# Layer-norm scaling as add of the negated mean and multiply, in place of subtract and multiply

## The chip, the cores and the metric

One core of a Trainium2 chip. The metric is the device time of one execution in microseconds; medians are over the fast runs of a kernel, and all runs told here were in the fast state (the one run timed only once has no state). TensorE, VectorE (DVE), ScalarE (ACT) and GpSimd (POOL) are separate engines. This kernel's program gives each of them a queue that is fixed beforehand, and lets them meet at semaphores (counters that one engine raises and another waits for). In the traces each engine works through its queue in order: the VectorE, ScalarE and GpSimd instructions of the kernel before stand in the same order in the first run told below, in which the long norm on GpSimd takes 821 ns in place of 2286.

## The reference, cut to what matters

Two layers, each an attention with a learned feature map followed by a gated MLP without a nonlinearity, both after a layer norm, on 2048 tokens of width 576 in bf16.

```python
def _layernorm(x, axis=-1, eps=1e-5):
    m = jnp.mean(x, axis=axis, keepdims=True)
    v = jnp.var(x, axis=axis, keepdims=True)
    return (x - m) / jnp.sqrt(v + eps)
...
    x = x + _A_ref(_layernorm(x, axis=-1), A_wqkv, A_w_phi, A_wo)      # attention; phi = softmax(p), softmax(-p) per head of 18
    x = x + _B_ref(_layernorm(x, axis=-1), B_w_gate, B_w_up, B_w_down) # (x Wg * x Wu) Wd, inner width 4608
    # ... and both once more
```

## The kernel before

Tokens are cut into 16 tiles of 128, taken in pairs ("blocks", eight of them). Work is written as small threads, and a list scheduler that runs when the program is built orders all instructions of all engines, using a duration that the author gave each operation.

A layer norm takes statistics on VectorE, `rstd = exp(-0.5 ln(var + eps))` on ScalarE, and then scales. The scaling is one of several alternatives; the scheduler takes the one that by its durations ends first. The last 64 columns are written twice (columns 576 to 639 repeat 512 to 575), hence two instructions per tile. (In all code here, "..." marks a cut.)

```python
boot = not fast and sig[0][0] == "xT" and sig[0][1] == 1      # the 16 norms at the start
...
em = [(lambda e, j=j, a=a, b=b, c=c: e.tensor_scalar(xln[:, sl[j], a:b], x_sb[:, ss[j], c:c + b - a],
        mv[:, sl[j], 0:1], rstd[:, sl[j]:sl[j] + 1], ALU.subtract, ALU.mult)) for a, b, c in ((0, 576, 0), (576, 640, 512))]
yield ("alt", [(eng, [Op(d, em[i], ...) for i, d in enumerate(dur)])
               for eng, dur in (("pool", (800, 200)), ("dve", (340, 100)))[:1 + fast]] + ([("act", act)] if boot else []))
```

So 42 of the norms in the gated stretches can only go to GpSimd, the 16 at the start to GpSimd or ScalarE, and six urgent ones (`fast`) to GpSimd or VectorE. GpSimd also forms a difference of the feature-map softmax (`dd<-psb,mxmn`) and its two products (`dd<-dd,ss`). VectorE also forms the softmax's row sums (`ss<-dd`) and the gated product (`hT<-ps,hT`), which empties the PSUM bank that TensorE needs for its next product:

```python
yield ("ops", "act", [Op(540, (lambda e, gb=gb, p=p: e.copy(hT[:, p, :], ps[:, gb, :])), ...)])
yield ("ops", "dve", [Op(625, (lambda e, ub=ub, p=p: e.tensor_tensor(hT[:, p, :], ps[:, ub, :], hT[:, p, :], ALU.mult)), ...)])
```

Of the kernel before, what the change touches and what calls it, by code (L numbers as in the profile page):

```python
# [7 lines left out]
F32 = mybir.dt.float32  # L8
ALU = mybir.AluOpType
ACTF = mybir.ActivationFunctionType  # L10
# [523 lines left out]
class K:  # L534
# [27 lines left out]
    def alloc(self):  # L562
        nc = self.nc
        A = lambda name, shape, dt: self.stack.enter_context(nc.sbuf_tensor(name, shape, dt))
        AT = lambda name, shape, dt, base: nc.alloc_sbuf_tensor_at(name, shape, dt, offset=base)
        self.ident = A("ident", [128, 128], BF16)
        self.epst = A("epst", [128, 1], F32)
        self.mask9 = A("mask9", [128, NK, GH], BF16)
        self.BD = A("BD", [128, NK, GH, CW], BF16)
        self.kvacc = A("kvacc", [128, NK, KW], F32)  # L570
        self.x_sb = A("x_sb", [128, NS, D], BF16)
        self.xT = A("xT", [128, 5, S], BF16)
        self.Wq = A("Wq", [128, 5, D], BF16)
        self.Wk = A("Wk", [128, 5, D], BF16)
        self.Wv = A("Wv", [128, 5, D], BF16)
        self.Wo = A("Wo", [128, 5, D], BF16)
        self.Wg = A("Wg", [128, 4, FF], BF16)
        self.Wu = A("Wu", [128, 4, FF], BF16)
        self.Wr = A("Wr", [128, FF], BF16)
        self.hT = A("hT", [128, NP, 512], BF16)  # L580
        h0 = nc.lookup_mloc(self.hT).addr
        self.Wraw = AT("Wraw", [128, 5, 2 * D], BF16, h0)
        self.WT = AT("WT", [TW, 2, NT, 128], BF16, h0 + 5 * 2 * D * 2)
        a0 = h0 + 5 * 2 * D * 2 + 2 * NT * 128 * 2
        self.BDphi = AT("BDphi", [TW, NT, TW], BF16, a0)
        self.onesf = AT("onesf", [128, 128], F32, a0 + 1280)
        self.wst = AT("wst", [TW, NT, DH], BF16, a0 + 1280 + 512)
        self.mask = AT("mask", [TW, TW], BF16, a0 + 1280 + 512 + 192)
        self.wdr = A("wdr", [128, self.NWD, CH, D], BF16)
        self.xln = A("xln", [128, 2 * self.NXP, 640], BF16)  # L590
        self.wdx = AT("wdx", [128, CH, D], BF16, nc.lookup_mloc(self.xln).addr + 2560)
        self.st = A("st", [128, 2 * self.NXP, 12], F32)
        self.mv = A("mv", [128, 2 * self.NXP, 2], F32)
        self.lnv = A("lnv", [128, 2 * self.NXP], F32)
        self.rstd = A("rstd", [128, 2 * self.NXP], F32)
        self.nmr = A("nmr", [128, 2 * self.NXP], F32)
        self.psb = A("psb", [128, self.NPS, D], BF16)
        self.mxmn = A("mxmn", [128, self.NPS, 2, H], F32)
        self.dd = A("dd", [128, self.NSM, 2, D], BF16)
        self.ss = A("ss", [128, self.NSM, 2 * H], F32)  # L600
        self.vx = A("vx", [128, self.NVX, H, CW], BF16)
        self.eT = A("eT", [128, self.NET, NK, 128], BF16)
        self.den = A("den", [128, self.NO, H], F32)
        self.oT = A("oT", [128, self.NOT, 5, 128], BF16)
        self.ps = self.stack.enter_context(nc.psum_tensor("ps", [128, 8, 512], F32))
        self.psb16 = [self.ps[:, i, :].bitcast(BF16) for i in range(8)]
        self.sbuf_left = nc.sbuf_bytes_remaining
        sc = self.sc
        sc.pool("xlnp", self.NXP)
        sc.pool("sm", self.NSM)  # L610
        sc.pool("psb", self.NPS)
        sc.pool("vx", self.NVX)
        sc.pool("et", self.NET)
        sc.pool("o", self.NO)
        sc.pool("oT", self.NOT)
        sc.pool("wt", 2)
        sc.pool("wd", self.NWD)
        sc.pool("pb", 8)
        self.vx_of = {}
        self.sm_of = {}  # L620
        self.wt_of = {}
        self.wd_slot = {}
        g = self.tr.dma_group
        self.g_wd = [g("wd%d" % i) for i in range(self.NWD + 1)]
        self.g_xt = [g("xt%d" % i) for i in range(2 * self.NXP)]
        self.g_out = g("out")
        self.g_et = [g("et%d" % i) for i in range(self.NET)]
        self.g_ot = [g("ot%d" % i) for i in range(self.NOT)]
        self.raw_keys = [("mask",), ("BDphi",), ("onesf",), ("wst",), ("WT", 0), ("WT", 1)] + [("Wraw", 0, w_, k_) for w_ in ("q", "k") for k_ in range(5)]
# [187 lines left out]
    def t_ln(self, tiles, sig, fast=False, slot=None):  # L817
        s = self
        x_sb, xln, st, mv, rstd, xT = s.x_sb, s.xln, s.st, s.mv, s.rstd, s.xT
        if slot is None:  # L820
            pair = yield ("acq", "xlnp")
            sl = [2 * pair, 2 * pair + 1]
        else:
            sl = [slot]
        n = len(tiles)
        js = range(n)
        key = lambda name: [(name, sl[j]) for j in js]
        ss = tiles
        ops = []
        for j in js:  # L830
            for h in range(2):
                ops.append(Op(d_dve(288), (lambda e, j=j, h=h: e.bn_stats(st[:, sl[j], 6 * h:6 * h + 6], x_sb[:, ss[j], 288 * h:288 * h + 288])),  # L832
                              reads=[("x", ss[j], 0), ("x", ss[j], 1)], writes=[("st", sl[j], h)]))
        yield ("ops", "dve", ops)
        ops = []
        for j in js:
            ops.append(Op(125, (lambda e, j=j: e.bn_aggr(mv[:, sl[j], :], st[:, sl[j], :])),
                          reads=[("st", sl[j], 0), ("st", sl[j], 1)], writes=[("mv", sl[j])]))
        yield ("ops", "dve", ops)
        s0, s1 = sl[0], sl[0] + n  # L840
        var2 = mv[:, s0:s1, 1:2].rearrange("p a b -> p (a b)")
        yield ("ops", "act", [
            Op(230, (lambda e: e.activation(s.lnv[:, s0:s1], var2, ACTF.Ln, bias=s.epst[:, 0:1], scale=1.0)),
               reads=key("mv") + [("epst",)], writes=key("lnv")),
            Op(205, (lambda e: e.activation(rstd[:, s0:s1], s.lnv[:, s0:s1], ACTF.Exp, scale=-0.5)),  # L845
               reads=key("lnv"), writes=key("rstd"))])
        boot = not fast and sig[0][0] == "xT" and sig[0][1] == 1
        if boot:
            mean2 = mv[:, s0:s1, 0:1].rearrange("p a b -> p (a b)")
            yield ("ops", "dve", [Op(80, (lambda e: e.scalar_tensor_tensor(s.nmr[:, s0:s1], mean2, -1.0, rstd[:, s0:s1], ALU.mult, ALU.mult)),  # L850
                                     reads=key("mv") + key("rstd"), writes=key("nmr"))])
        for j in js:
            act = [Op(d, (lambda e, j=j, a=a, b=b, c=c: e.activation(xln[:, sl[j], a:b], x_sb[:, ss[j], c:c + b - a], ACTF.Identity,
                                                                     bias=s.nmr[:, sl[j]:sl[j] + 1], scale=rstd[:, sl[j]:sl[j] + 1])),
                      reads=[("x", ss[j], 0), ("x", ss[j], 1), ("nmr", sl[j]), ("rstd", sl[j])], writes=[("xln", sl[j])]) for a, b, c, d in ((0, 576, 0, 760), (576, 640, 512, 330))]
            em = [(lambda e, j=j, a=a, b=b, c=c: e.tensor_scalar(xln[:, sl[j], a:b], x_sb[:, ss[j], c:c + b - a], mv[:, sl[j], 0:1], rstd[:, sl[j]:sl[j] + 1],  # L856
                                                                 ALU.subtract, ALU.mult)) for a, b, c in ((0, 576, 0), (576, 640, 512))]
            yield ("alt", [(eng, [Op(d, em[i], reads=[("x", ss[j], 0), ("x", ss[j], 1), ("mv", sl[j]), ("rstd", sl[j])], writes=[("xln", sl[j])]) for i, d in enumerate(dur)])
                           for eng, dur in (("pool", (800, 200)), ("dve", (340, 100)))[:1 + fast]] + ([("act", act)] if boot else []))
        for j in js:  # L860
            tok = slice(128 * ss[j], 128 * ss[j] + 128)
            if fast:
# [3 lines left out]
                                        reads=[("xln", sl[j]), ("ident",)], writes=[("pbd", bank)], excl=[("pb", bank)]) for k in range(5)])  # L866
                yield ("ops", "act", [Op(d_act(640, True), (lambda e, P=P, tok=tok: e.copy(xT[:, :, tok], P[:, 0:640].rearrange("p (k n) -> p k n", k=5))),  # L867
                                         reads=[("pbd", bank)], writes=[("xT", ss[j])], excl=[("pb", bank)])])
# [662 lines left out]
```

## Time and profile before

| | before |
|---|---|
| device time | 1173.97 us (1172.96 to 1175.02, three runs) |
| TensorE, VectorE, ScalarE, GpSimd busy | 1091.9, 612.2, 376.1, 361.5 us |
| start, to the first gated matmul | 130.1 us |
| gated stretch of layer 1 | 523.0 us |
| hand-over and layer 2 | 37.2 + 482.8 us |

The last three rows are read from the trace: the first matmul of the gated MLP, and the first residual add on VectorE after the last block of a layer. The stages fit the windows view, whose columns are the stretch, its length, and then the busy microseconds of TensorE, its weight loads, VectorE, ScalarE and GpSimd. Kernel before:

```profile
130.10:653.10 523.00, 515.69 (x7651) 400.36 (x7652) 279.36 (x567) 163.94 (x376) 181.63 (x146) 1.00 0.43 104
653.10:690.30 37.20, 20.00 (x156) 14.20 (x154) 28.12 (x65) 13.13 (x30) 6.95 (x6) 0.79 0.08 25
690.30:1173.10 482.80, 470.49 (x6972) 361.91 (x6972) 202.96 (x411) 116.19 (x238) 86.94 (x70) 0.99 0.43 109
```

The gated stretches show TensorE idle for 7.3 and 12.3 us only.

### The profile page before, as it was taken

Reading aid. Unit: us, or ns where it says so; the run is one execution under the profiler, and the core shown is the slowest. Engines: PE = TensorE matmul, PEld = TensorE weight load, DVE = VectorE, ACT = ScalarE, POOL = GpSimd, SP = SyncE. Lnnn points to the kernel's source line nnn. Section 1 sums busy time; section 2 is a strip of 40 time slices with the busy share of each in tenths; the row PEclk is TensorE's granted clock in tenths of the full one; section 3 lists DMA queues with packets and bytes.
Section 4 is the critical chain, followed back from the end, with each engine's and each line's share of the span. In section 5 each row is a group of like instructions: output and inputs, shape, how many; then the busy total and the mean of one; then the engine's idle time right before and its main releaser. Section 6 shows DMA issues by size and latency. Waiting matters only on the chain.

```text
span 1173.1 us, 34065 instructions
## 1 busy us (share of the span) xinstructions
PE 1091.9 (93%) x15480; PEld 838.8 (72%) x15480; DVE 612.2 (52%) x1262; ACT 376.1 (32%) x857; POOL 361.5 (31%) x301
## 2 busy tenths in 40 slices
PE   5676899999999999999999589999999999999998
PEld 3554686868778686868777368586868686868685
DVE  6787654646547364736544565462626262534131
ACT  6685331423324151413322232131303131312120
POOL 7885223415344251515331121230403030301000
PEclk9897899999999999999999889999999999999999
DMA  6384118253362727254442301817273535354414
GB/s 170 80 273 169 21 25 219 40 158 71 94 132 45 185 34 193 40 157 68 102 114 69 115 10 31 230 23 200 37 187 51 167 69 150 79 140 97 148 47 132
DMA packets 181034, 128.24 MB, mean 109 GB/s; under 512 B 99354, under 2 KB 179738, under 8 KB 179738
## 3 DMA queue, kind: packets, MB, share of 16 engines
q1 hardware_dynamic: 180890, 126.07, 42.3%
q8 instruction: 121, 1.98, 0.7%
q14 instruction: 23, 0.19, 0.1%
HBM read 100.73 MB, written 2.36 MB: 88 GB/s over the span
## 4 chain that ended last, share of the span: by engine, by line
PE 64%; POOL 12%; DVE 12%; ACT 5%; DMA 4%; issue 1%; SPq 0%; DVEq 0%; POOLq 0%
PE ps L1232 31%; PE ps L1302 19%; POOL xln L856 7%; PE ps L898 6%; DVE ss L965 3%; POOL dd L976 3%; DMA wdr<-in_B_w_down_dram 3%; PE ps L1305 3%; POOL dd L935 3%; PE ps L886 2%; PE ps L1131 2%; DVE x_sb L1179 2%; DVE hT L1280 2%; ACT dd L960 1%; PE ps L1017 1%
## 5 line engine op out<-in xcount | busy, mean ns | idle before, releaser
L1232 PE MATMUL ps<-xT,Wu 64*128 64x256 bf16 x4608 | 592.2, 270 | 6.6 <-DVE hT L1280 5.6
L1232 PE MATMUL ps<-xT,Wg 64*128 64x256 bf16 x4608 | 590.5, 270 | 1.6 <-ACT xT L867 1.6
L1232 PEld LDWEIGHTS ps<-xT,Wu 64*128 64x128 bf16 x4608 | 432.1, 94 | 32.7 <-DVE hT L1280 11.7
L1232 PEld LDWEIGHTS ps<-xT,Wg 64*128 64x128 bf16 x4608 | 426.9, 94 | 30.5 <-issue 3.3
L1278 ACT CAST hT<-ps 128x512 bf16<-128x512 f32 x288 | 166.5, 583 | 545.3 <-PE ps L1232 508.4
L1280 DVE TENSOR_TENSOR hT<-ps,hT 128x512 bf16<-128x512 f32 x288 | 196.6, 688 | 203.6 <-ACT hT L1278 203.1
L856 POOL TENSOR_SCALAR xln<-x_sb,mv,rstd 128x576 bf16<-128x576 bf16 x102 | 145.5, 1432 | 464.0 <-ACT rstd L845 458.9
L1302 PE MATMUL ps<-wdr,hT 128*128 128x512 bf16 x960 | 247.8, 380 | 4.3 <-DMA wdr<-in_B_w_down_dram 3.9
L1232 PE MATMUL ps<-xT,Wr 64*128 64x256 bf16 x1152 | 199.0, 271 | 0.0
L1305 PE MATMUL ps<-wdr,hT 128*128 128x64 bf16 x960 | 185.0, 193 | 1.4 <-ACT hT L1278 1.4
L976 POOL TENSOR_TENSOR dd<-dd,ss 128x576 bf16<-128x576 bf16 x124 | 142.9, 1174 | 129.1 <-ACT ss L972 124.4
L1302 PEld LDWEIGHTS ps<-wdr,hT 128*128 128x128 bf16 x960 | 93.8, 98 | 115.0 <-DMA wdr<-in_B_w_down_dram 7.3
L1327 DVE TENSOR_TENSOR x_sb<-ps,x_sb 128x512 bf16<-128x512 f32 x32 | 21.9, 685 | 199.5 <-PE ps L1305 199.5
L965 DVE TENSOR_REDUCE ss<-dd 128x64 f32<-128x1152 bf16 x64 | 86.2, 1347 | 56.3 <-ACT dd L960 56.0
L935 POOL TENSOR_TENSOR dd<-psb,mxmn 128x576 bf16<-128x576 bf16 x62 | 72.1, 1163 | 122.9 <-DVE mxmn L925 122.9
L1305 PEld LDWEIGHTS ps<-wdr,hT 128*128 128x128 bf16 x960 | 94.0, 98 | 2.0 <-ACT hT L1278 2.0
L1232 PEld LDWEIGHTS ps<-xT,Wr 64*128 64x128 bf16 x1152 | 89.6, 95 | 5.6
L958 ACT ACTIVATE dd<-dd 128x576 bf16<-128x576 bf16 x64 | 43.7, 683 | 65.3 <-DVE dd L944 65.2
L925 DVE TENSOR_REDUCE mxmn<-psb 128x32 f32<-128x576 bf16 x64 | 47.3, 739 | 21.1 <-ACT psb L922 21.1
L922 ACT CAST psb<-ps 128x288 bf16<-128x288 f32 x128 | 46.8, 399 | 33.7 <-PE ps L886 22.8
L1302 PE MATMUL ps<-wdx,hT 128*128 128x512 bf16 x192 | 53.5, 380 | 0.0
L832 DVE BATCH_NORM_STATS2 st<-x_sb 128x6 f32<-128x288 bf16 x128 | 49.3, 445 | 5.7 <-DMA x_sb<-in_A_x_dram 5.4
(85 smaller groups left out, 944.7 us busy)
## 6 DMA issues: line engine op xcount, KB each, us to landing
wdr<-in_B_w_down_dram SPq DMA_DIRECT2D x240, 288.0 KB, 3.7
wdx<-in_B_w_down_dram SPq DMA_DIRECT2D x48, 288.0 KB, 3.6
Wg<-in_B_w_gate_dram SPq DMA_DIRECT2D x4, 1152.0 KB, 12.5
Wu<-in_B_w_up_dram SPq DMA_DIRECT2D x4, 1152.0 KB, 15.3
x_sb<-in_A_x_dram SPq DMA_DIRECT2D x8, 288.0 KB, 3.3
out_dram<-x_sb SPq DMA_DIRECT2D x16, 144.0 KB, 2.3
Wraw<-in_A_wqkv_dram SPq DMA_DIRECT2D x8, 144.0 KB, 3.2
xT<-xln SPq DMA_TRANSPOSE x58, 2.6
```

What stands on the lines that cost most here:

```text
L832: ops.append(Op(d_dve(288), (lambda e, j=j, h=h: e.bn_stats(st[:, sl[j], 6 * h:6 * h + 6], x_sb[:, ss[j], 288 * h:288 * h + 288])), reads= ...
L856: em = [(lambda e, j=j, a=a, b=b, c=c: e.tensor_scalar(xln[:, sl[j], a:b], x_sb[:, ss[j], c:c + b - a], mv[:, sl[j], 0:1], rstd[:, sl[j]:s ...
L898: out.append(Op(61, (lambda e, h=h, k=k, st=(i == 0 and k == 0), sp=(i == 1 and k == 3): e.matmul(s.ps[:, banks[h], 0:N], L[r, k, :], Wm[r ...
L925: ops = [Op(665, (lambda e: e.tensor_reduce(mxmn[:, pz, 0, :], p3, AX.X, ALU.max)), reads=[("psb", pz, 0), ("psb", pz, 1)], writes=[("mx", ...
L935: yield ("alt", [(eng, [Op(dur, (lambda e: e.tensor_tensor(d1, p3, mxb, ALU.subtract)), reads=[("psb", pz, 0), ("psb", pz, 1), ("mx", pz)] ...
L965: Op(1320, (lambda e: e.tensor_reduce(ss[:, sm, :].rearrange("p (b g) -> p b g", b=2), e4, AX.X, ALU.add)), reads=s.ddk(sm, 0) + s.ddk(sm, ...
L976: yield ("alt", [(eng, [Op(dur, (lambda e, ev=ev, rb=rb: e.tensor_tensor(ev, ev, rb, ALU.mult)), reads=s.ddk(sm, br) + [("ss", sm)], write ...
L1232: out.append(Op(54.3, (lambda e, bank=bank, cs=cs, lhsT=lhsT, rhs=rhs, st=st, sp=sp: e.matmul(ps[:, bank, cs], lhsT, rhs, start=st, stop=s ...
L1278: yield ("ops", "act", [Op(540, (lambda e, gb=gb, p=p: e.copy(hT[:, p, :], ps[:, gb, :])), reads=[("gu", gb)], writes=[("hT", p)] + (s.raw ...
L1280: yield ("ops", "dve", [Op(625, (lambda e, ub=ub, p=p: e.tensor_tensor(hT[:, p, :], ps[:, ub, :], hT[:, p, :], ALU.mult)), reads=[("gu", u ...
L1302: ops.append(Op(d_pe(512), (lambda e, lhsT=lhsT, bank=bank, slot=slot, fi=fi, f=f: e.matmul(ps[:, bank, 0:512], lhsT, s.wslot(slot)[:, fi, ...
L1305: ops.append(Op(d_pe(64) + 3, (lambda e, lhsT=lhsT, sl=sl, slot=slot, fi=fi, f=f: e.matmul(ps[:, Z, 64 * sl:64 * sl + 64], lhsT, s.wslot(s ...
```

## The change

The intent: the same value by another pair of operations, `(x + (-m)) * rstd`. The negation is a small new VectorE instruction that runs while ScalarE computes rstd. At the start, ScalarE's alternative makes its own bias and copies the tail instead of computing it twice, and its durations are raised from 760 + 330 to 180 + 860 + 240 ns. GpSimd's durations stay at 800 and 200.

```diff
+        self.nmean = A("nmean", [128, 2 * self.NXP], F32)
...
+        mean2 = mv[:, s0:s1, 0:1].rearrange("p a b -> p (a b)")
+        yield ("ops", "dve", [Op(80, (lambda e: e.tensor_scalar(s.nmean[:, s0:s1], mean2, -1.0, None, ALU.mult)), ...)])
...
-        if boot:
-            ... nmr = -mean * rstd by scalar_tensor_tensor on VectorE
...
-            act = [... two ACTF.Identity activations, durations 760 and 330 ...]
-            em = [... e.tensor_scalar(..., mv[:, sl[j], 0:1], rstd[:, sl[j]:sl[j] + 1], ALU.subtract, ALU.mult) ...]
+            act = [Op(180, ... ACTF.Copy, nmr = nmean * rstd ...), Op(860, ... ACTF.Identity, 576 columns ...),
+                   Op(240, (lambda e, j=j: e.copy(xln[:, sl[j], 576:640], xln[:, sl[j], 512:576])), ...)]
+            em = [... e.tensor_scalar(..., s.nmean[:, sl[j]:sl[j] + 1], rstd[:, sl[j]:sl[j] + 1], ALU.add, ALU.mult) ...]
```

(Lines with "..." inside are cut.)

More of the change, by code (lines that the diff above doesn't have):

```diff
@@ L841, in t_ln @@
         var2 = mv[:, s0:s1, 1:2].rearrange("p a b -> p (a b)")
+        mean2 = mv[:, s0:s1, 0:1].rearrange("p a b -> p (a b)")
+        yield ("ops", "dve", [Op(80, (lambda e: e.tensor_scalar(s.nmean[:, s0:s1], mean2, -1.0, None, ALU.mult)), reads=key("mv"), writes=key("nmean"))])
         yield ("ops", "act", [
@@ L847, in t_ln @@
         boot = not fast and sig[0][0] == "xT" and sig[0][1] == 1
-        if boot:
-            mean2 = mv[:, s0:s1, 0:1].rearrange("p a b -> p (a b)")
-            yield ("ops", "dve", [Op(80, (lambda e: e.scalar_tensor_tensor(s.nmr[:, s0:s1], mean2, -1.0, rstd[:, s0:s1], ALU.mult, ALU.mult)),
-                                     reads=key("mv") + key("rstd"), writes=key("nmr"))])
         for j in js:
-            act = [Op(d, (lambda e, j=j, a=a, b=b, c=c: e.activation(xln[:, sl[j], a:b], x_sb[:, ss[j], c:c + b - a], ACTF.Identity,
-                                                                     bias=s.nmr[:, sl[j]:sl[j] + 1], scale=rstd[:, sl[j]:sl[j] + 1])),
-                      reads=[("x", ss[j], 0), ("x", ss[j], 1), ("nmr", sl[j]), ("rstd", sl[j])], writes=[("xln", sl[j])]) for a, b, c, d in ((0, 576, 0, 760), (576, 640, 512, 330))]
-            em = [(lambda e, j=j, a=a, b=b, c=c: e.tensor_scalar(xln[:, sl[j], a:b], x_sb[:, ss[j], c:c + b - a], mv[:, sl[j], 0:1], rstd[:, sl[j]:sl[j] + 1],
-                                                                 ALU.subtract, ALU.mult)) for a, b, c in ((0, 576, 0), (576, 640, 512))]
-            yield ("alt", [(eng, [Op(d, em[i], reads=[("x", ss[j], 0), ("x", ss[j], 1), ("mv", sl[j]), ("rstd", sl[j])], writes=[("xln", sl[j])]) for i, d in enumerate(dur)])
@@ new lines, in t_ln @@
+            xr = [("x", ss[j], 0), ("x", ss[j], 1)]
+            act = [Op(180, (lambda e, j=j: e.activation(s.nmr[:, sl[j]:sl[j] + 1], s.nmean[:, sl[j]:sl[j] + 1], ACTF.Copy, scale=rstd[:, sl[j]:sl[j] + 1])),
+                      reads=[("nmean", sl[j]), ("rstd", sl[j])], writes=[("nmr", sl[j])]),
+                   Op(860, (lambda e, j=j: e.activation(xln[:, sl[j], 0:576], x_sb[:, ss[j], :], ACTF.Identity,
+                                                        bias=s.nmr[:, sl[j]:sl[j] + 1], scale=rstd[:, sl[j]:sl[j] + 1])),
+                      reads=xr + [("nmr", sl[j]), ("rstd", sl[j])], writes=[("xln", sl[j])]),
+                   Op(240, (lambda e, j=j: e.copy(xln[:, sl[j], 576:640], xln[:, sl[j], 512:576])), reads=[("xln", sl[j])], writes=[("xln", sl[j])])]
@@ L859, in t_ln @@
+            em = [(lambda e, j=j, a=a, b=b, c=c: e.tensor_scalar(xln[:, sl[j], a:b], x_sb[:, ss[j], c:c + b - a], s.nmean[:, sl[j]:sl[j] + 1], rstd[:, sl[j]:sl[j] + 1],
+                                                                 ALU.add, ALU.mult)) for a, b, c in ((0, 576, 0), (576, 640, 512))]
+            yield ("alt", [(eng, [Op(d, em[i], reads=[("x", ss[j], 0), ("x", ss[j], 1), ("nmean", sl[j]), ("rstd", sl[j])], writes=[("xln", sl[j])]) for i, d in enumerate(dur)])
                            for eng, dur in (("pool", (800, 200)), ("dve", (340, 100)))[:1 + fast]] + ([("act", act)] if boot else []))
```

## The prediction

> **What bounds the kernel now.** I read the page first (busy shares and slices), then cut the run into its stages with the windows view, then the waits of TensorE stage by stage, then the GpSimd groups kept apart by shape, and last the chain of waits through the first 132 us.
>
> ```profile
> PE 1091.9 (93%) x15480; PEld 838.8 (72%) x15480; DVE 612.2 (52%) x1262; ACT 376.1 (32%) x857; POOL 361.5 (31%) x301
> ...
> PE   5676899999999999999999589999999999999998
> ```
>
> TensorE is busy 93% of 1173.1 us, and the slices show two places where it is not full: the first five slices (the first attention layer's key side, where the layer norms of all 16 token tiles lie) and the 23rd and 24th (the hand-over between the two layers).
>
> ```profile
> core 0: us, PE busy (x) PEld busy (x) DVE busy (x) ACT busy (x) POOL busy (x), PEclk, DMA share, GB/s
> 0.00:30.00 30.00, 16.17 (x110) 11.27 (x110) 20.68 (x62) 20.11 (x51) 21.37 (x26) 1.00 0.69 169
> 30.00:60.00 30.00, 21.46 (x180) 15.88 (x181) 23.55 (x49) 20.94 (x58) 25.35 (x23) 0.89 0.35 81
> 60.00:100.00 40.00, 29.57 (x277) 22.10 (x275) 35.86 (x67) 29.45 (x79) 30.83 (x27) 0.97 0.88 314
> 100.00:130.00 30.00, 18.49 (x141) 13.07 (x139) 21.57 (x48) 12.30 (x28) 8.34 (x7) 0.73 0.03 8
> 130.00:390.00 260.00, 255.28 (x3809) 199.30 (x3810) 146.53 (x304) 83.21 (x191) 93.90 (x76) 0.99 0.42 99
> 390.00:652.00 262.00, 259.35 (x3837) 200.55 (x3836) 132.93 (x262) 80.74 (x186) 87.83 (x70) 1.00 0.45 107
> 652.00:692.00 40.00, 22.75 (x182) 15.91 (x182) 29.82 (x69) 13.13 (x30) 8.43 (x7) 0.78 0.10 32
> ```
>
> After the stretch come TensorE's busy time and the others'. TensorE is idle 44.3 us in the first 130 (13.8 + 8.5 + 10.4 + 11.5), 17.3 us in 652 to 692, and only 81.1 - 44.3 - 17.3 = 19.5 us in the remaining 1003. So the four stretches of the gated MLP leave almost nothing to win; the start is the place. There GpSimd is the busiest engine in the first 60 us (46.7 of 60), and VectorE from 60 to 100 (35.9 of 40).
>
> ```profile
> L976 POOL TENSOR_TENSOR dd<-dd,ss 128x576 bf16<-128x576 bf16 x124 | 142.9, 1174 | 129.1 <-ACT ss L972 124.4 <-DVE ss L969 4.7
> L856 POOL TENSOR_SCALAR xln<-x_sb,mv,rstd 128x576 bf16<-128x576 bf16 x51 | 116.6, 2286 | 458.9 <-ACT rstd L845 458.9
> L935 POOL TENSOR_TENSOR dd<-psb,mxmn 128x576 bf16<-128x576 bf16 x62 | 72.1, 1163 | 122.9 <-DVE mxmn L925 122.9
> L856 POOL TENSOR_SCALAR xln<-x_sb,mv,rstd 128x64 bf16<-128x64 bf16 x51 | 29.5, 578 | 5.0
> ```
>
> The layer norm's own line is the second and fourth: 2286 ns for 576 elements, 578 ns for the 64-column tail. It is twice as slow as the products and differences of two tensors of the same size (1174, 1163 ns), although it reads only one tensor.
>
> ```profile
> 8.50 2.29 POOL xln L856
> ...
> 10.89 2.85 POOL xln L856 x2
> ...
> 27.10 2.30 POOL xln L856
> ...
> 65.77 2.28 POOL xln L856
> ```
>
> These pieces of the chain of waits, with their 0.58 us tails (three more pieces, and a fourth inside the 2.85), are 11.5 us of the first 132 us: 8.7% by the view's own sum.
>
> **What the Trainium skill says.** "GPSIMD Engine Reference", section 3.1, gives about 2.6 cycles an element for a two-input operation, and its section 4.1 calls one-input operations "roughly line-rate". The trace agrees with the first: 1163 ns over 576 elements at the 1.2 GHz of that page is 2.4 cycles. It disagrees with the second: (2286 - 578) / (576 - 64) = 3.34 ns an element, 4.0 cycles. So this one-input instruction is on some slow path. Neither page nor trace says whether the subtract, the two operations or the two per-partition operands put it there. "ScalarE: Activation LUTs", section "What ACT_TABLE_LOAD costs", gives 186 ns + 0.833 ns an element, plus about 93 ns for each per-partition operand: 852 ns for 576 elements with two, 425 ns for 64. The trace has 865 and 438 ns on seven tiles. "VectorE: DVE Perf Modes", section on the errata, says that small operations pay a fixed latency per instruction; here the smallest nmr (two columns) takes 143 ns, which I take for the new negation.
>
> **The change part by part.**
> 1. GpSimd, 51 tiles: subtract and multiply become add and multiply, nothing else about the instruction. This can only be meant for a faster instruction. The program's own duration for the pair is 800 and 200 ns, unchanged by the edit, whereas its 1150 for the two-tensor operations matches the trace. A slope of (800 - 200) / 512 = 1.17 ns is what a path without the penalty would look like. I judge it 70% likely that the add pair is fast, near 1.0 us and 0.3 us (estimate, between the program's figure and the two-tensor time): 1.3 instead of 2.86 us a tile, 1.55 us less, 79 us of GpSimd over the run.
> 2. What of it lies on the path. In the gated stretches TensorE's idle time is the limit: 19.5 us in all, none of it put down to these instructions. The shorter norms there mostly add slack: 1 us. At the hand-over the norms run on VectorE (six tiles, 426 + 300 ns): unchanged, 0. At the start the chain holds four tiles, 4 x 1.55 = 6.2 us. Part of it comes back. The first keys wait for their weights until 15.0 us whatever the norm does. VectorE, at 36 of 40 us from 60 to 100, cannot follow a faster GpSimd there. I keep about two thirds: 4 us. To this comes the pile of six multiplications at 31.1 us, which waits behind the norms and holds TensorE for 4.35 us until 33.5: another 1 us at most. Sum with the gated stretches: about 6 us less.
> 3. VectorE: 35 negations (29 of two tiles, 6 of one) less the 8 products at the start are 27 more small instructions; at 0.15 us this is 4 us of 612. Each runs while ScalarE does logarithm and exponential (0.30 + 0.21 us) that the norm waits for anyway. On the path: 0.
> 4. ScalarE at the start: the bias product moves there (about 0.2 us a tile), the tail becomes a plain copy (estimate 0.24 by the skill's rule, not 0.44). Even per tile, apart from two waits on itself. But the program's estimate for this alternative rises from 1090 to 1280 ns against GpSimd's 1000, so its list scheduler will probably give some of ScalarE's seven tiles to GpSimd. With a fast GpSimd that costs nothing; with a slow one each tile moved adds 2.86 us to the busiest engine of the first 60 us, on the path perhaps 1 to 2 us each.
> 5. The instruction order comes from that scheduler, so new durations reshuffle the order of all engines, from the first tile on. The parameters were tuned for the old order. I put +1 us on it, with several us of spread either way.
>
> Sum, GpSimd fast: -6 + 1 = -5, 1169 us. GpSimd not fast: +3 + 1, 1178 us.
>
> **The rivals.**
> (a) The add is no faster on GpSimd. For it: there the two-tensor subtract and multiply cost the same (1163 and 1174 ns), so the kind of arithmetic does not show in that form; the slow path could come from the two per-partition operands, which stay. Against it: a change with no other purpose, and the 800/200 in the program. Time: 1174 to 1182.
> (b) GpSimd is fast, but the start is held by VectorE: it is busy 101.7 of the first 130 us, and the transposes, loads and weights queue. For it: the fullest stretch of all is VectorE's, 60 to 100. Then the gain is the first 40 us' alone, 2 to 3 us: 1171.
> (c) GpSimd is fast and the whole start tightens, since the scheduler's model now fits the chip: TensorE's 44.3 us of idle time shrink by a quarter to a third: 1160. Against it: VectorE's 101.7 us plus the fixed head and the serial hand-over at 100 to 130 leave hardly more than 12 us.
> (d) The reshuffle costs more than the faster norm gives: a stall on a buffer or bank in the gated stretches, 5 to 10 us. Nothing in the trace speaks for it in particular.
>
> **Range and chances.** Weighting 1169 (0.7) and 1178 (0.3) gives 1171.7; since the fast branch is the mode, I predict 1170 us, with 1159 to 1180 for 8 times in 10: the lower edge is rival (c), the upper rival (a) with moved tiles. A gain of 2% is 23.5 us, above half of all idle TensorE time at the start and more than the rest of the start allows: 0.04. A loss of 2% needs a broken order: 0.03. Within 2%: 0.93.
>
> **What will show it.** Right: the GpSimd row for the 576-element norm falls to 0.8 to 1.2 us and its tail to 0.2 to 0.4; GpSimd's busy time falls by some 80 us to 280; the norm leaves the chain at the start; the long TensorE run of the gated stage starts 3 to 7 us before 130; the gated stretches keep their lengths within 2 us each; VectorE's norm rows stay at 426 and 300 ns. Wrong: a GpSimd row still at 2.29 us (step 1 falls); the row fast but the gated stage no earlier (step 2 falls, rival b); the gain or loss lying after 130 us (step 5 was mis-sized); more than nine tiles of the start on GpSimd with a later start (step 4).

## The result, and the profile after

| | before | after |
|---|---|---|
| device time | 1173.47 us (1171.38 to 1175.02, four runs) | 1154.31 us (1151.23 to 1157.23, four runs) |
| ratio | 1 | 0.9837, 95% interval 0.9804 to 0.9871 |
| start | 130.1 us | 121.1 us |
| gated stretch of layer 1 | 523.0 us | 514.7 us |
| hand-over and layer 2 | 37.2 + 482.8 us | 37.5 + 476.2 us |

A ratio here and below is the mean time of one kernel's fast runs over that of the other's in the same rounds, so it is not quite the ratio of the medians beside it. The kernel became 19 us faster, below the range (1159 to 1180). The profiled run of the changed kernel was its fastest; its stages add up to 23.6 us less than before's.

The GpSimd rows of the norm, changed kernel, shapes apart (busy us in all, mean ns of one):

```profile
L859 POOL TENSOR_SCALAR xln<-x_sb,nmean,rstd 128x576 bf16<-128x576 bf16 x52 | 42.7, 820 | 408.7 <-ACT rstd L848 358.7 <-DVE nmean L844 43.6 <-DVE Wk L809 5.9
L859 POOL TENSOR_SCALAR xln<-x_sb,nmean,rstd 128x64 bf16<-128x64 bf16 x52 | 20.4, 393 | 5.2
```

2286 ns became 820, 578 became 393: 1.65 us less per tile. The two rows together are 83.0 us shorter, though they hold one tile more; all of GpSimd is 80.4 us less busy (361.5 - 281.1), as it also has one more softmax difference. The stages of the changed kernel:

```profile
121.10:635.80 514.70, 511.79 (x7651) 400.09 (x7652) 283.69 (x581) 164.33 (x376) 135.96 (x146) 1.00 0.44 105
635.80:673.30 37.50, 20.35 (x156) 14.18 (x154) 28.49 (x68) 13.23 (x30) 6.67 (x6) 0.82 0.08 25
673.30:1149.50 476.20, 468.90 (x6972) 363.34 (x6972) 206.25 (x419) 117.38 (x239) 64.37 (x70) 0.99 0.42 111
```

The same number of matmuls (7651, 6972) now takes 8.3 and 6.6 us less. Of these 14.9 us, 9.4 are idle time (7.3 to 2.9 and 12.3 to 7.3), and 5.5 were counted as busy (515.7 to 511.8 and 470.5 to 468.9). So the busy row had hidden part of the holding, but not all of the 5.5 us is that: in the first 20 us of layer 1's gated stretch TensorE is busy throughout in both profiles (20.00 us), yet runs 340 matmuls after and 320 before, at a granted clock of 0.93 and 0.88. Some 1.2 us (estimate: 20 matmuls of 59 ns each) are thus the clock's. In layer 2's blocks, at 1.00 in both, 0.2 of the 0.6 us gained per block were counted as busy (59.51 to 59.33).

What held TensorE is in the chain of waits, in 12 of the 16 blocks (six in each layer). Here is one block of layer 2 in the kernel before, start and length in us (the last piece ends with the window asked for, 952 to 972):

```profile
952.42 0.21 ACT rstd L845
...
952.73 2.29 POOL xln L856
...
955.11 2.85 POOL xln L856 x2
...
958.05 0.58 POOL xln L856
958.63 1.14 POOL dd L935
...
959.79 0.69 ACT dd L960
...
960.50 1.36 DVE ss L965
...
966.66 1.35 DVE ss L965
968.01 0.61 DVE hT L1280
...
968.67 3.34 PE ps L1232 x57
```

Read it from the bottom. TensorE starts again at 968.67 when the gated product has emptied its bank. That product stood in VectorE's queue behind a row sum, the row sum waited for an exponential, which goes back by a second round of the same steps to a softmax difference on GpSimd (L935), and that one stood in GpSimd's queue behind 5.9 us of layer norm for a quite different pair of tiles. The corresponding place after the change (window 998 to 1008):

```profile
998.00 2.90 PE ps L1235 x52
1000.89 0.58 ACT hT L1281
...
1001.50 0.69 DVE hT L1283
1002.19 0.74 DVE dd L947 x2
...
1004.24 1.35 DVE ss L968
1005.59 0.61 DVE hT L1283
...
1006.25 1.81 PE ps L1235 x29
```

Here the chain no longer passes GpSimd; only what follows directly from TensorE's own last products is left in it. The block takes 59.8 us instead of 60.4 (from residual add to residual add). In the shares over the whole span GpSimd's part of the chain fell from 12% to:

```profile
PE 83%; DVE 9%; ACT 4%; DMA 3%; POOL 1%; issue 1%; SPq 0%; DVEq 0%; ACTq 0%
```

### The profile page after: what moved, and what is told of

It is laid out like the page before. It is cut to its first block, busy times and chain, and to the rows that moved or that the text cites. A ratio compares the mean times of both kernels' runs of the same rounds, so it can differ in the third digit from the quotient of the medians.

```text
span 1149.5 us, 34128 instructions
## 1 busy us (share of the span) xinstructions
PE 1082.6 (94%) x15480; PEld 837.1 (73%) x15480; DVE 618.8 (54%) x1289; ACT 376.9 (33%) x860; POOL 281.1 (24%) x304
## 4 chain that ended last, share of the span: by engine, by line
PE 83%; DVE 9%; ACT 4%; DMA 3%; POOL 1%; issue 1%; SPq 0%; DVEq 0%; ACTq 0%
PE ps L1235 44%; PE ps L1305 20%; PE ps L901 9%; PE ps L1308 3%; PE ps L889 2%; PE ps L1134 2%; DVE ss L968 2%; DMA wdr<-in_B_w_down_dram 2%; PE ps L1020 1%; DVE x_sb L1182 1%; POOL dd L979 1%; DVE mxmn L928 1%; DVE mxmn L933 1%; DVE hT L1283 1%; DVE dd L947 1%
## 5 line engine op out<-in xcount | busy, mean ns | idle before, releaser
L979 POOL TENSOR_TENSOR dd<-dd,ss 128x576 bf16<-128x576 bf16 x124 | 143.7, 1180 | 148.7 <-ACT ss L975 144.9
L859 POOL TENSOR_SCALAR xln<-x_sb,nmean,rstd 128x576 bf16<-128x576 bf16 x104 | 62.6, 607 | 413.8 <-ACT rstd L848 358.7
L925 ACT CAST psb<-ps 128x288 bf16<-128x288 f32 x128 | 47.4, 400 | 37.5 <-PE ps L901 20.5
L933 DVE TENSOR_REDUCE mxmn<-ps 128x16 f32<-128x288 f32 x128 | 52.0, 448 | 0.0
```

Of the source, the lines that this page charges most:

```text
L933: ops.append(Op(370, (lambda e, h=h, pv=pv: e.tensor_reduce(mxmn[:, pz, 1, 16 * h:16 * h + 16], pv, AX.X, ALU.min)), reads=[("pbd", bank)] ...
L979: yield ("alt", [(eng, [Op(dur, (lambda e, ev=ev, rb=rb: e.tensor_tensor(ev, ev, rb, ALU.mult)), reads=s.ddk(sm, br) + [("ss", sm)], write ...
```

## The experiments

The theory after the result: the faster instruction alone does it (its speed), at the start and, through the in-order queues, in the gated blocks. The rivals: the new order of the schedule did much of it; or the speed does not come from add in place of subtract. The stage lengths are collected in one table below. The kernels ran on three chips, each beside its own runs of the kernel before: the first four told here (old order with add, new order with subtract, add in a part) beside 1176.86 us; the two repeats, the changed kernel with true durations and the single instructions beside 1174.9; the other four beside 1174.11.

### Speed and order, taken apart

Old order with add; the result is wrong, since the mean is added:

```diff
-  mv[:, sl[j], 0:1], rstd[:, sl[j]:sl[j] + 1], ALU.subtract, ALU.mult
+  mv[:, sl[j], 0:1], rstd[:, sl[j]:sl[j] + 1], ALU.add, ALU.mult
```

The instructions of all engines were compared with before's and stand in the same order.

> The kernel before with one word changed: the layer norm on GpSimd (and the six on VectorE) adds the mean instead of subtracting it. Wrong result on purpose; order, waits and counts of every engine are those of before. If the speed of the GpSimd instruction is the whole cause: its rows at 820 and 393 ns as in the changed kernel, and 1155 us (ratio 0.981 to 0.988). If the new order of the schedule gave much of the gain: rows just as fast, but only 1163 to 1168 us, the gain at the start alone. If the speed does not come from add in place of subtract: rows at 2286 and 578 ns and 1173 us.

Measured: rows at 821 and 393 ns, 1158.77 us, ratio 0.9845 (0.9818 to 0.9872). The speed alone gives 1.5%.

New order with subtract (the changed kernel, `ALU.add` back to `ALU.subtract`, also wrong):

> The changed kernel with one word changed back: the layer norm subtracts the negated mean. Wrong result on purpose; order and waits are those of the changed kernel. If speed is the whole cause: rows at 2286 and 578 ns and 1173 to 1180 us (one more tile of the start on GpSimd than before, so rather a little above before). If the order gave much of the gain: 1160 to 1168 us.

Measured: rows at 2287 and 579 ns, 1169.61 us, ratio 0.9934 (0.9908 to 0.996). Neither expectation was met squarely: it is below before, so the new order (with the rest of the edit: the negations, and ScalarE's own bias and copied tail) is worth 0.7% to the slow instruction. To the fast one it is worth less by the times, as the repeat of both on one chip shows:

> The changed kernel once more, on one chip with the next run, so that the order's share is read without a change of chip. Speed alone: the two within 0.3% of each other. If the new order adds to the speed: the changed kernel 3 us or more below the next run.

> The old order with add (wrong result on purpose), again, beside the changed kernel: ratio 0.984 to 0.986 to the kernel before. Speed alone: within 0.3% of the changed kernel.

Measured: 1153.99 us, ratio 0.9825 (0.98 to 0.9849), for the changed kernel; 1157.39 us, ratio 0.9847 (0.9827 to 0.9866), for the old order with add. They are 0.2% apart with intervals that overlap: of the 1.75%, 1.53 are the instruction's speed, and at most the rest, some 3 us, is order.

### Start and gated stretches, taken apart

The kernel before with add in a part of the norms:

```diff
+        op0 = ALU.add if boot else ALU.subtract      # start only; the other run has the two exchanged
...
-  ALU.subtract, ALU.mult
+  op0, ALU.mult
```

> The kernel before, with add only in the 16 norms of the start (nine of them on GpSimd), subtract in the others; order of before. My prediction's terms (start 5 us, rest 1): 1168 us. If the traces' stage limits are right (start 9.0 us shorter, the gated stretches 8.3 and 6.6): 1164 us, and the gated stretches as long as before.

Measured: 1170.13 us, ratio 0.9943 (0.9919 to 0.9966): 6.7 us (0.57% of 1176.86). The start's term of the prediction, 5 us, was about right. Its output is wrong, which doesn't matter for the time.

> The kernel before, with subtract in the norms of the start and add in all others; order of before. By my prediction's terms: 1172 us. If the norm's time in every block of the gated stretches reaches TensorE (through GpSimd's next instruction, the row sum on VectorE behind it and the eviction queued behind that): 1158 to 1160 us, start unchanged at 130 us, the hold of TensorE at the product of each block (0.6 us per block) gone.

Measured: 1163.2 us, ratio 0.9882 (0.9854 to 0.991): 13.9 us. The output passed the comparison though the mean has the wrong sign in these norms. So two thirds of the gain lie where the prediction had put 1 us. The two parts sum to 1.75% and together gave 1.53 to 1.55%.

### Is it GpSimd's queue?

The kernel before, subtract and all, with the gated norms on VectorE:

```diff
-  for eng, dur in (("pool", (800, 200)), ("dve", (340, 100)))[:1 + fast]]
+  for eng, dur in ((("pool", (800, 200)),) if boot else (("dve", (340, 100)),))]
```

TensorE's, ScalarE's and the DMA queue's orders are exactly before's; VectorE now has 36.1 us of norms (48 tiles, six of them as before) and GpSimd loses its 42.

> The kernel before, subtract in all norms, but the 42 norms of the gated stretches on VectorE instead of GpSimd (right result). TensorE's and ScalarE's orders are exactly those of before. If what costs is GpSimd's queue, held for 5.7 us per pair of norms so that the softmax's next difference comes late: about as good as add in the gated stretches alone, 1160 to 1166 us, start unchanged near 130 us. If any engine that runs the norm passes its time on to TensorE, or VectorE's extra 30 us do: 1172 us or more.

Measured: 1159.95 us, ratio 0.9883 (0.9865 to 0.9901), the same as add in the gated stretches alone. VectorE can take the work without passing it on to TensorE. So it was the place in GpSimd's queue that cost. By itself this run leaves a rival, since the norm also ends sooner (0.75 us on VectorE against 2.86). Against the rival stand the chain above, which goes from the norm to GpSimd's next instruction and not to the norm's own readers, and the view of the tile `xln` in the kernel before, in which the projections inside the gated stretches (L898) wait for the norm's output once, for 0.3 us. The next run settles it: there the norm stays on GpSimd and stays slow.

### Would a schedule that knew have hidden it?

The kernel before with one pair of numbers changed, and the slow instruction kept:

```diff
-  (("pool", (800, 200)), ("dve", (340, 100)))
+  (("pool", (2290, 580)), ("dve", (340, 100)))
```

> The kernel before, subtract and all, with the scheduler told the true durations of the slow norm (2290 and 580 ns instead of 800 and 200). If a schedule that knows how slow the instruction is can hide it: 1168 us or less. If its time is on the path whatever the order: 1173 us or more; the reshuffle seen in the run with true durations of the fast norm (10 us later at the start) says that the start may move either way by that much, so the stages must be read one by one: gated stretch of layer 1 near 522 us if it cannot be hidden, near 515 if it can.

Measured: 1160.73 us, ratio 0.9889 (0.9859 to 0.992), with rows still at 2286 and 579 ns. The start is no shorter (132.6 us, with three of its norms on GpSimd and 13 on ScalarE, where there were nine and seven), the gated stretch of layer 1 is 515.0 us. How it is hidden is seen on VectorE. The kernel before, one block of layer 2 (start, length, count, and idle time before it with what ended it):

```profile
963.16 1.28 DVE L1280 TENSOR_TENSOR hT<-ps,hT 128x512 bf16<-128x512 f32 x2
964.36 0.81 DVE L944 TENSOR_TENSOR dd<-ps,mxmn 128x288 bf16<-128x288 f32 x2
966.66 1.35 DVE L965 TENSOR_REDUCE ss<-dd 128x64 f32<-128x1152 bf16 x1 [1.50 <-ACT dd L960]
967.93 1.28 DVE L1280 TENSOR_TENSOR hT<-ps,hT 128x512 bf16<-128x512 f32 x2
```

The kernel that was told the true durations, a block of layer 2:

```profile
954.36 0.81 DVE L944 TENSOR_TENSOR dd<-ps,mxmn 128x288 bf16<-128x288 f32 x2
955.97 0.69 DVE L1280 TENSOR_TENSOR hT<-ps,hT 128x512 bf16<-128x512 f32 x1 [0.80 <-ACT hT L1278]
957.03 0.69 DVE L1280 TENSOR_TENSOR hT<-ps,hT 128x512 bf16<-128x512 f32 x1 [0.37 <-ACT hT L1278]
957.64 1.34 DVE L965 TENSOR_REDUCE ss<-dd 128x64 f32<-128x1152 bf16 x1
```

Before, the row sum stands in front of two gated products and makes them wait 1.50 us for an operand that is late. With true durations the two products come first, and the row sum then finds its operand ready. Other queues changed too (GpSimd now forms the second difference at 953.20, ahead of the first one's two products at 954.32; before, it came after them, at 964.75 after 962.51), and the run does not tell the changes apart. So the slow instruction need not have cost anything in the gated stretches: it cost there because the queues were ordered for a fast one.

### Numbers and variants of the changed kernel

The changed kernel with `("pool", (820, 390))`, the durations now measured:

> The changed kernel with the scheduler told the measured durations of the GpSimd norm (820 and 390 ns instead of 800 and 200). If the program's schedule still suffers from that error: 2 to 4 us below the changed kernel; if not: within 3 us of it, in either direction, which would be the size of a mere reshuffle.

Measured: 1164.24 us, ratio 0.9904 (0.9888 to 0.992). A miss: 10 us worse. The gated stretches are the changed kernel's (514.5 us in layer 1); all the loss is at the start, which takes 133.5 us instead of 121 to 123. The next run has a like result:

> The changed kernel without the ScalarE alternative: all 16 norms of the start on the fast GpSimd. My step 4 said that tiles moved to a fast GpSimd cost nothing: within 4 us of the changed kernel. If ScalarE's share matters at the start: 5 us or more above it. Gated stretches as in the changed kernel (515 and about 509 us).

(The change is the removal of the ScalarE alternative, `+ ([("act", act)] if boot else [])`.) Measured: 1160.68 us, ratio 0.9885 (0.9869 to 0.99), against 0.9825 of the changed kernel on its chip; the start takes 129.0 us, the rest is the changed kernel's. By the time this is another miss of mine. But the windows of the start say where the 7.9 us lie: TensorE is idle there as long as in the changed kernel (39.7 us against 39.5); it is its busy time that grew, from 81.6 to 89.3 us for the same matmuls, at a granted clock of 0.86 against 0.93. That ratio alone would make 81.6 us into 88.2 (estimate). So this run does not show that the moved tiles were in the way. The lower clock goes with this kernel, not with one run: over the whole span it is 0.972 or 0.973 in all four runs, and 0.979 to 0.981 in the four of the kernel told next, on the same chip. Why stays open. The run before this one is different: there TensorE's idle time at the start is 7.3 us longer (46.8 us), and the clock is lower too (0.88).

> The changed kernel with the gated norms on VectorE too; a try at a version better than both. If GpSimd's remaining 1.2 us per norm still hold anything: 1146 to 1152 us. If nothing is left to win there: 1153 to 1158 us.

(The same edit as for the norms on VectorE above, made to the changed kernel.) Measured: 1154.06 us, ratio 0.9831 (0.9815 to 0.9848): as the changed kernel. Nothing is left for the norm to give in the gated stretches, and no version here beats the changed kernel.

### The instruction by itself

24 GpSimd instructions were added after the changed kernel's last, twelve forms twice, each running alone after the one ahead of it:

```diff
+ forms = [lambda e: e.tensor_scalar(Y, X, m, r, ALU.subtract, ALU.mult),
+          lambda e: e.tensor_scalar(Y, X, m, r, ALU.add, ALU.mult), ...]
```

> The changed kernel with 24 further GpSimd instructions after its last one, 128x576 bf16, twelve forms twice: pairs (subtract, multiply), (add, multiply), (multiply, add), (multiply, subtract), (add, subtract), (add, add), (max, multiply) with two per-partition operands; subtract, add, multiply alone; the first two pairs with immediates. If subtract is slow as such: every form with it near 2.3 us, also alone. If only some pairs have a fast path: (add, multiply) and few others at 0.8 us, the rest of the pairs slow. If the per-partition operands made it slow: the pair with immediates fast with either operation.

Groups of that run, costliest first, busy us in all and then the mean ns of one. The line numbers stand for: 1489 (subtract, multiply), 1490 (add, multiply), 1491 (multiply, add), 1494 add alone, 1497 (add, add), 1499 (subtract, multiply) with immediates, 1500 (add, multiply) with immediates.

```profile
L1497 POOL TENSOR_SCALAR psb<-Wq,nmean,rstd 128x576 bf16<-128x576 bf16 x2 | 4.6, 2294 | 0.2
...
L1489 POOL TENSOR_SCALAR psb<-Wq,nmean,rstd 128x576 bf16<-128x576 bf16 x2 | 4.6, 2291 | 0.1
...
L1499 POOL TENSOR_SCALAR psb<-Wq 128x576 bf16<-128x576 bf16 x2 | 4.3, 2140 | 0.2
...
L1494 POOL TENSOR_SCALAR psb<-Wq,nmean 128x576 bf16<-128x576 bf16 x2 | 3.5, 1728 | 0.2
...
L1491 POOL TENSOR_SCALAR psb<-Wq,rstd,nmean 128x576 bf16<-128x576 bf16 x2 | 1.7, 826 | 0.2
L1490 POOL TENSOR_SCALAR psb<-Wq,nmean,rstd 128x576 bf16<-128x576 bf16 x2 | 1.6, 824 | 0.2
L1500 POOL TENSOR_SCALAR psb<-Wq 128x576 bf16<-128x576 bf16 x2 | 1.3, 672 | 0.2
```

It is not subtract that is slow. (add, multiply) and (multiply, add) are fast, and everything else tried is slow: (add, add) 2294, (multiply, subtract) 2293, (max, multiply) 2290, (add, subtract) 2288, and even add, subtract or multiply alone take 1727 to 1728 ns, twice as long as the fast pair. The per-partition operands add about 150 ns to either pair (824 - 672, 2291 - 2140) and are not the cause.

### The stages of all runs

From the profiles, in us: to the first gated matmul, with TensorE's idle time and the mean granted clock in it by the windows view in brackets; from there to the first residual add after layer 1's last block; from there to the same in layer 2's last block (hand-over included).

| kernel | start (idle, clock) | layer 1 gated | to layer 2's end |
|---|---|---|---|
| before | 130.1 (44.4, 0.90) | 523.0 | 515.4 |
| changed, two profiles | 121.1 (39.5, 0.93), 122.9 (39.5, 0.91) | 514.7, 515.0 | 509.3, 510.5 |
| add, old order, two profiles | 127.0 (41.4, 0.90), 123.4 (42.1, 0.90) | 515.3, 516.0 | 511.2, 510.4 |
| subtract, new order | 129.4 (42.6, 0.89) | 521.0 | 514.1 |
| add at the start only | 123.6 (41.4, 0.93) | 522.3 | 515.8 |
| add in the gated stretches only | 132.3 (44.9, 0.85) | 516.0 | 509.6 |
| gated norms on VectorE, subtract | 130.4 (44.4, 0.87) | 515.4 | 510.6 |
| before, true durations | 132.6 (47.0, 0.90) | 515.0 | 508.3 |
| changed, true durations | 133.5 (46.8, 0.88) | 514.5 | 509.8 |
| changed, no norm on ScalarE | 129.0 (39.7, 0.86) | 516.4 | 509.7 |
| changed, gated norms on VectorE | 121.0 (39.3, 0.93) | 515.5 | 510.8 |
| changed, 24 instructions at its end | 121.2 (39.6, 0.93) | 513.7 | 509.0 |

The start scatters: the same order with the slow norm gives 130.1, 130.4 and 132.3 us, with the fast norm 123.4, 123.6 and 127.0. Their means, 130.9 and 124.7, are 6.3 us apart; the new order with the fast norm has 122.0 as the mean of its two. TensorE's idle time in the start scatters much less, and parts the four cases: 44.4 to 44.9 us (old order, slow norm), 41.4 to 42.1 (old, fast), 42.6 (new, slow), 39.3 to 39.6 (new, fast). By it the fast norm is worth 3 us at the start in either order, and the new order 2 us with either norm. The rest of the differences lies in TensorE's busy time, where the granted clock differs as well; no run holds the clock fixed, so how much of that rest the change itself brings is not shown. The reading of the gated stretches hardly depends on this: add there alone, at the clock of the kernel before (1.00 in both in layer 1), has 516.0 us against 523.0. The second and third columns fall in two groups each: 521 to 523 or 514 to 516, 514 to 516 or 508 to 511.

## Why the prediction was wrong, point by point

- The intent and step 1 were right. The add pair is fast; 820 and 393 ns against the estimated 1.0 and 0.3 us. GpSimd's busy time is 281.1 us against "some 80 us to 280". Rival (a), no faster add, is refuted by the rows.
- **Step 2 failed, in its term for the gated stretches: "The shorter norms there mostly add slack: 1 us".** Measured 13.9 us with add there alone, and 14.9 us between the two traces' stages. The step argued from TensorE's idle time, "19.5 us in all, none of it put down to these instructions". Both halves of it misled. A wait is put down to the last link, here the gated product on VectorE (5.6 us on the page before); that link had been made late by one that was two engines away. And 5.5 of the 14.9 us were inside TensorE's busy time (some 1.2 of them the clock's). The chain of waits had it in plain view: its norm on GpSimd was 6.8% of the whole span by that view's own figure, with a piece in 12 of the 16 blocks. The prediction read the chain only up to 132 us. Its list of signs put a gain after 130 us down to step 5; the run with the old order shows that it belongs to step 2. (A slip without effect: the idle time in all is 81.2 us, not 81.1.)
- Step 2's term for the start, 4 + 1 us, was right in size: 6.7 us with add there alone (4.0 to 9.5 by the interval), and the norm left the chain there, as foretold. But only 3 us of it are idle time of TensorE, with which the step reckoned; the rest is busy time at a mostly higher granted clock, so the agreement may be partly luck. The pile of six multiplications starts at 28.2 to 28.8 us with add in the old order, not at 31.1, more than the 1 us allowed for it; what reached TensorE of that, and of VectorE's fullness, no run tests. Rival (b) called for a start held by VectorE and 2 to 3 us; it was more.
- Step 3 held as far as it is tested: 27 more instructions on VectorE (1289 against 1262), median 169 ns where 150 was assumed, and the hand-over is 37.5 us against 37.2. "On the path: 0" was nearly right: two negations stand in the changed kernel's chain at the start, with 0.54 and 0.07 us. (Of the six urgent tiles, which step 2 put at the hand-over, two lie at the end of the start.)
- Step 4 was right on the move, by one tile (six on ScalarE instead of seven). ScalarE's bias product takes 295 ns, not 200, its plain tail copy 244 as estimated. "With a fast GpSimd that costs nothing" is open: without any norm on ScalarE the start takes 129.0 us, but TensorE's idle time in it is the same, and the clock is lower.
- Step 5, +1 us for the new order, has the wrong sign: the new order is better by 7 to 8 us (0.66%) with the slow norm, and by some 3 us with the fast one, where the intervals overlap but TensorE's idle time at the start points the same way (2 us). Its "several us of spread either way" is real: 121 to 133 us at the start among orders of the fast norm.
- Rival (c), 1160 us by a tighter start, named the right cause, a scheduler model that now fits the chip, but in the wrong place. Rival (d), a stall in the gated stretches, did not come: they got shorter.

## What to carry to other kernels

A long instruction on an engine that is mostly idle can hold the busiest engine by way of in-order queues. Follow the chain of waits through every stage, and do not take the idle time of the busiest engine, or the name of its last waker, for the limit of what a distant engine costs. Where two runs of a stage differ, split it into idle and busy time and look at the granted clock before naming a cause. Where a scheduler orders the queues, compare its durations with the profile's rows first: one that was 2.9 times too low cost 1.1% here, all of it in the gated stretches, and there a true number cured it as well as a faster instruction did. On GpSimd, write a scaling like this one (128x576, bf16) as add and multiply, and measure any other pair.

## What the Trainium skill lacked or had wrong

- "GPSIMD Engine Reference", section 4.1, calls one-input operations roughly line-rate. For the 128x576 bf16 tile on two per-partition operands that holds, of the forms tried, for the pairs (add, multiply) and (multiply, add) alone (824 and 826 ns): for the first (820 - 393) / 512 = 0.83 ns an element, one cycle at the 1.2 GHz that the page gives. For (subtract, multiply) it is 3.34 ns, and four more pairs and three single operations stand at 1727 to 2294 ns against 824. No page tells these apart.
- The same page, section 3.1, has a two-input operation at about 2.6 cycles an element, which is close here (1163 ns for 576, 2.4 cycles). So one slow one-input instruction (2286 ns) costs twice a two-input one, which the page's order of costs would not let one expect.
- "ScalarE: Activation LUTs", section "What ACT_TABLE_LOAD costs": right within 15 ns for both scalings (865 and 438 ns against 852 and 425) and for the plain tail copy (244 ns against 239).
- No page says that an operation alone can be slower on GpSimd than the pair that contains it: add alone 1728 ns, add and multiply 824 ns.
